# First-layer weights as three pieces of whole rows right behind the first chunk pair, one half-row pair, and a new order of all steps

## The chip, the cores and the metric

The kernel runs on one core of one Trainium2 chip. The metric is device time in microseconds. Three runs of the kernel before gave 149.23, 148.55 and 149.03 us; their median, 149.03 us, is the time before.

## The reference

Two layers are fused. The first is a linear attention with a decaying state: 4 batches, 8 heads, 768 time steps, head width 48.

```python
for t in range(S):
    cur = einsum('bhd,bhe->bhde', u * k[t], v[t])
    y[:, :, t] = einsum('bhd,bhde->bhe', r[t], state + cur)
    state = w * state + einsum('bhd,bhe->bhde', k[t], v[t])
```

Its output, laid out as x with 4 x 768 rows of 384 columns, goes through a layer norm and two dense layers with a residual:

```python
xn = (x - mean(x)) / sqrt(var(x) + 1e-06) * g_ln
out = x + maximum(xn @ w_ch1, 0) @ w_ch2      # 384 -> 1536 -> 384
```

All inputs and the output are float32; the matrix products run in bf16.

## The kernel before

The 3072 rows are cut into 24 chunks of 128 time steps, six to a batch. Two neighbouring chunks form a pair (12 pairs). The recurrence is turned into matrix products within a chunk, with a state `Z` carried from chunk to chunk.

The program is a list of steps, `PLAN`, written out by hand. Each entry is a step's name, its number and a letter for the engine (v is DVE, s is ACT, g is POOL, - stands where the step's engine is fixed). Every engine works through its own steps strictly in the order of this list, and so does the queue of SP, which issues nearly all loads and stores. Which engine waits for which data follows from the list and from the number of buffers (`SLOTS`).

The steps that matter here:

- `LK2`, `LR2`, `LV2` load a pair of k, r or v (384 KB) so that two neighbouring time steps lie in one row; `LK`, `LR`, `LV` load one chunk (192 KB). For the first `PAIRS` pairs the whole attention works on pairs laid out in such half rows (`AT2`, `Y2`, `AM2`), later pairs on single chunks (`AT`, `Y`, `AM`).
- `LN` takes the logarithm of the decay w on ACT, `WBM` spreads it over the partitions on PE, and `FR2`, `FK2`, `FR`, `FK` make tables of decay powers from it with Exp on ACT. `TL` loads an ACT table set that holds both functions: `nc.scalar.preload_act_table_set("natural_log_exp_and_others")`.
- `SK`, `SR` (and `SKH`, `SRH`, `SR2`) multiply k and r by the decay powers; `TRk`, `TRr` transpose them on PE (the pairs from number 4 on by DMA, `TDk`), `TCk`, `TCr` copy the results out of PSUM; `AT` makes the scores, `AM` masks them on DVE, `S` updates the state, `Y` gives the chunk's output, `X` completes it, `XN` normalises, `LT` and `XT` (or `LTD`, by DMA) transpose it.
- `LW1` loads the first layer's weights, `SW` scales a third of a third of them by the norm's gain into bf16 tiles `w1_sb[n][kc]`. `IW2` loads the second layer's weights on POOL's own queue. `UP` is a block of first-layer products (12 matmuls for a single chunk, 6 wide ones for a double one), `RL` the relu that takes it out of PSUM (two buffers `hp`), `DN` a third of a chunk's second-layer products, `OT` the residual, `STO` the store.
- `RS` makes the norm's factor of a chunk: on POOL with a power, or on ACT with Ln and then Exp (lines 613 and 614).
- `DU` are matmuls on zeros that feed nothing.

A tile `w1_f[n]` holds the columns of one third n of the hidden units, for all three blocks kc of the 384 input columns, so `UP,n` of a single chunk needs the one load `LW1,n`.

Of the kernel before, what the change touches and what calls it, by code (L numbers as in the profile page):

```python
# [7 lines left out]
FP32 = mybir.dt.float32  # L8
# [11 lines left out]
LN,0,s MI2,0,g MP,5,g MP,3,g WBM,0,- MP,4,g LG,0,- MM,0,g LV2,0,- DU,4096,- UWR,0,v FR2,0,s MI,0,g FR2,1,s LR2,2,- SRH,0,v  # L20
FK2,0,s SRH,1,v FK2,1,s SKH,0,v LK,5,- FK,0,s TRr,0,- SKH,1,v DU,1024,- TCr,0,s SR2,1,v TRk,0,- LR2,3,- DU,512,- SK2,1,v COL,0,-
TCk,0,s TRr,1,- LV2,1,- CV2,0,s UW,0,v Q2,0,v AT2,0,- DU,1536,- FR,0,s TCr,1,v LK,4,- WL,0,s SR2,2,g AM2,0,v S,0,- AT2,1,-
LK,6,- CC2,0,s DU,512,- ZU,0,v TRk,1,- AM2,1,v DU,512,- VB2,0,g S,1,- TCk,1,s LK,7,- DU,512,- TRr,2,- LW1,1,- SR2,3,v DU,512,-
Y2,1,- TCr,2,s LW1,2,- LV,5,- Q2,1,v Y2,0,- SK,4,g ZU,1,v UGC,0,s LV,4,- CV2,1,s X,1,v TRr,3,- SK,5,g X,0,v DU,512,-
AT2,3,- TCr,3,s DU,512,- AM2,3,v SK,7,g S,2,- XN,1,s AT2,2,- XN,0,g CC2,1,v ZU,2,v SQ,1,s DU,512,- VB2,1,g TRk,2,- AM2,2,v
S,3,- LW1,0,- TCk,2,s DU,512,- SK,6,v LT,1,- Y2,2,- SQ,0,s SW,5,g XT,1,v SW,3,s LV,6,- LT,0,- SW,4,v TRk,3,- Q2,2,g
ZU,3,v DU,1024,- SW,6,s LK,8,- XT,0,v Y2,3,- SW,7,s TCk,3,v X,2,v SW,8,s AT,5,- AT,4,- X,3,v XN,2,g DU,512,- UP,2,-
AM,5,v XN,3,s IW2,0,g LV,7,- UP,1,- RL,2,s Q2,3,g AM,4,v LT,2,- CV2,2,s DU,512,- UP,17,- RL,1,s XT,2,v S,4,- RL,17,s
LR2,4,- UP,34,- SW,0,v SW,2,s AT,6,- CC2,2,v ZU,4,v SW,1,s VB2,2,g AT,7,- AM,6,v LK,9,- Y,4,- RL,34,s UP,0,- IW2,1,g
X,4,v UP,18,- RL,0,s AM,7,v IW2,2,g Y,5,- XN,4,s LT,3,- UP,32,- RL,18,s RS,1,g LV,8,- X,5,v LT,4,- UP,33,- RL,32,s  # L30
XT,3,v XN,5,g DU,512,- CV2,3,v LV,9,- UP,16,- RL,33,s XT,4,v SK,8,v S,6,- DN,0,- SR2,4,v CC2,3,s RL,16,s UP,48,- SQ,5,s
ZU,6,v UP,64,- VB2,3,v RL,48,s TRr,4,- SQ,3,s Y,6,- SK,9,g DN,1,- RS,3,s X,6,v RL,64,s UP,66,- RS,0,g TDk,4,- SQ,2,s
DN,2,- RS,2,g LT,5,- S,7,- OT,0,v RL,66,s UP,49,- XN,6,s XT,5,v UP,50,- RL,49,v TCr,4,s LR2,6,- DN,4,- ZU,7,v UP,80,-
ZD,7,v LK,10,- CV2,4,g RL,50,v Y,7,- RL,80,s DN,5,- X,7,v LV,13,- DN,6,- Q2,4,v XN,7,s UP,65,- SQ,4,s OT,1,v LV,11,-
AT,8,- SQ,6,s SR2,6,v AT,9,- DN,8,- RS,6,s LR2,5,- AM,8,v RS,4,s DN,9,- SQ,7,s LK,11,- S,8,- DN,10,- ZU,8,v LV,10,-
UP,82,- CC2,4,s OT,2,v VB2,4,g LK,12,- LT,6,- AM,9,v Y,8,- RL,82,s DN,12,- STO,0,- RL,65,s SK,10,g DN,13,- XT,6,v LK,13,-
X,8,v DN,14,- ZD,8,g LV,12,- S,9,- UP,96,- OT,3,v SK,11,g ZU,9,v UP,98,- RL,96,s SR2,5,v Y,9,- TDk,5,- SQ,8,s DN,16,-
CV2,5,v LT,7,- TRr,5,- SK,12,v DN,17,- X,9,v TCr,5,s RL,98,v LK,15,- UP,97,- XN,9,g LK,14,- XT,7,v ZD,9,g UP,81,- RL,97,s
LR2,7,- XN,8,s SK,13,g UP,112,- RL,81,s LTD,8,- DN,18,- RS,7,s Q2,5,v TRr,6,- OT,4,v UP,114,- SK,15,g TCr,6,s RL,112,v STO,1,-
S,10,- CV2,6,g DN,20,- CC2,5,s TDk,6,- RL,114,s SK,14,v AT,10,- RS,5,s AT,11,- ZU,10,v DN,21,- SR2,7,g AM,10,v UP,113,- STO,3,-  # L40
DN,22,- AM,11,v RL,113,s TDk,7,- Y,10,- VB2,5,g UP,129,- OT,5,v TRr,7,- RL,129,s LR,19,- UP,130,- ZD,10,g X,10,v UP,133,- LV,14,-
# [29 lines left out]
def kernel(  # L71
# [31 lines left out]
    const = ctx.enter_context(tc.tile_pool(name="const", bufs=1))  # L103
# [82 lines left out]
    g_neg = const.tile([P, CK], FP32, name="g_neg")  # L186
    WLZ = const.tile([P, HP, E2], FP32, name="WLZ")
    uwI = const.tile([P, HP, 2], BF16, name="uwI")
    w1_f = [const.tile([P, CK, FW], FP32, name=f"w1_f{n}") for n in range(NW)]
    w1_sb = [[const.tile([P, FW], BF16, name=f"w1_sb{n}_{kc}") for kc in range(CK)] for n in range(NW)]  # L190
    w2_sb = [const.tile([P, FK // NW, C], BF16, name=f"w2_sb{n}") for n in range(NW)]
    w1_src = moe_w_ch1.rearrange("(kc p) (n f) -> p n kc f", p=P, n=NW)
    w2_src = moe_w_ch2.rearrange("(n p fk) c -> p n fk c", p=P, n=NW)

    psum = {}
# [135 lines left out]
                func=ACT.Exp, scale=float(L),  # L331
            )

    def LW1(n, e):
        nc.sync.dma_start(out=w1_f[n][:], in_=w1_src[:, n])

    def SW(i, e):
        n, kc = divmod(i, CK)
        o, s = w1_sb[n][kc][:], w1_f[n][:, kc]
        g = g_neg[:, kc : kc + 1]  # L340
        if e == "s":
            nc.scalar.activation(out=o, in_=s, func=ACT.Copy, scale=g)  # L342
        elif e == "v":
            nc.vector.tensor_scalar(out=o, in0=s, scalar1=g, scalar2=None, op0=ALU.mult)
        else:
            nc.gpsimd.tensor_scalar(out=o, in0=s, scalar1=g, scalar2=1.0, op0=ALU.mult, op1=ALU.mult)
# [436 lines left out]
```

## Time and profile before

| what | value |
|---|---|
| median of three runs | 149.03 us |
| span of the profiled execution | 147.5 us |
| PE busy | 141.5 us (96%) |
| DVE busy | 112.3 us (76%) |
| ACT busy | 82.4 us (56%) |
| POOL busy | 72.0 us (49%) |
| moved by DMA | 27.18 MB |
| granted TensorE clock | 1.000 |

The profile gives the span of the execution that it recorded, 147.5 us from the first to the last instruction, and no time of its own for what lies around it; the median is 1.53 us above that span. A busy PE in this profile is not PE at its peak: overlapping matmuls count as one busy stretch, and the matmuls on zeros count too.

### The profile page before, as it was taken

Reading aid. Unit: us, or ns where it says so; the run is one execution under the profiler, and the core shown is the slowest. Engines: PE = TensorE matmul, PEld = TensorE weight load, DVE = VectorE, ACT = ScalarE, POOL = GpSimd, SP = SyncE. Lnnn points to the kernel's source line nnn. Section 1 sums busy time; section 2 is a strip of 40 time slices with the busy share of each in tenths; the row PEclk is TensorE's granted clock in tenths of the full one; section 3 lists DMA queues with packets and bytes.
Section 4 is the critical chain, followed back from the end, with each engine's and each line's share of the span. In section 5 each row is a group of like instructions: output and inputs, shape, how many; then the busy total and the mean of one; then the engine's idle time right before and its main releaser. Section 6 shows DMA issues by size and latency. Waiting matters only on the chain.

```text
span 147.5 us, 4689 instructions
## 1 busy us (share of the span) xinstructions
PE 141.5 (96%) x1943; PEld 111.1 (75%) x1943; DVE 112.3 (76%) x206; ACT 82.4 (56%) x181; POOL 72.0 (49%) x96
## 2 busy tenths in 40 slices
PE   7899999799999999999999999999999999999991
PEld 3375767699987788787778787778877777878881
DVE  3499999889559887998989999499644886851642
ACT  4657783986977737736766543115795164537010
POOL 7507687984070475794854194627129330614000
PEclk9999999999999999999999999999999999999999
DMA  4999997999959899999899997998959894213023
GB/s 112 300 242 240 192 339 187 283 243 215 220 95 231 202 225 165 264 205 258 164 192 196 195 235 124 173 204 227 197 112 191 182 142 154 82 46 119 8 99 111
DMA packets 85097, 27.18 MB, mean 184 GB/s; under 512 B 80338, under 2 KB 83540, under 8 KB 85076
## 3 DMA queue, kind: packets, MB, share of 16 engines
q1 hardware_dynamic: 84642, 25.70, 78.3%
q0 software_dynamic: 432, 1.18, 4.3%
q8 instruction: 15, 0.25, 0.7%
q14 instruction: 6, 0.05, 0.1%
q10 hardware_dynamic: 2, 0.00, 0.0%
HBM read 18.88 MB, written 4.72 MB: 160 GB/s over the span
## 4 chain that ended last, share of the span: by engine, by line
PE 65%; SPq 13%; DMA 11%; DVE 6%; POOL 1%; issue 1%; DVEq 0%
PE o L674 28%; PE hp L646 25%; DMA kf<-in_k_dram 6%; DMA w_f<-in_moe_w_ch_dram 5%; SPq L374 4%; SPq L352 3%; PE at L544 3%; PE y L583 2%; SPq L358 2%; PE y L481 2%; PE y L575 2%; SPq L371 1%; SPq L377 1%; DVE hT L664 1%; PE y L460 1%
## 5 line engine op out<-in xcount | busy, mean ns | idle before, releaser
L646 PE MATMUL hp<-xT,w_sb 128*128 128x128 bf16 (+1 forms) x648 | 57.1, 237 | 0.8 <-ACT w_sb L342 0.7
L662 ACT ACTIVATE hT<-hp 128x512 bf16<-128x512 f32 x55 | 32.4, 594 | 40.5 <-PE hp L646 39.7
L646 PEld LDWEIGHTS <-w_sb 128*128 128x128 bf16 x648 | 49.3, 114 | 5.1 <-ACT w_sb L342 1.3
L674 PE MATMUL o<-w_sb,hT 128*128 128x384 bf16 x276 | 53.0, 326 | 0.0
L674 PEld LDWEIGHTS <-hT 128*128 128x128 bf16 x276 | 25.0, 97 | 12.0
L553 DVE TENSOR_TENSOR A<-at,mask 128x1024 bf16<-128x1024 f32 x20 | 24.2, 1216 | 2.1 <-PE at L544 2.1
L492 POOL TENSOR_TENSOR Vb<-vf,cc 128x768 f32<-128x768 f32 x11 | 16.5, 1498 | 14.9 <-ACT cc L200 8.5
L730 DVE SCALAR_TENSOR_TENSOR ot<-o,rs,x 128x384 f32<-128x384 f32 x23 | 14.1, 615 | 12.3 <-PE o L674 7.0
L205 POOL TENSOR_TENSOR sk<-kf,Fk 128x384 bf16<-128x384 f32 x13 | 13.6, 1053 | 8.5 <-DMA kf<-in_k_dram 7.9
L597 ACT ACTIVATE sqj<-x,sm 128x384 bf16<-128x384 f32 x24 | 14.6, 609 | 2.2 <-DVE x L590 2.2
L205 POOL TENSOR_TENSOR Z<-ZS,WLZ 128x384 bf16<-128x384 f32 x8 | 8.0, 1002 | 15.4 <-DVE ZS L565 15.4
L590 DVE SCALAR_TENSOR_TENSOR x<-y,Vb 128x384 f32<-128x384 f32 x20 | 11.0, 552 | 4.5 <-PE y L583 4.1
L664 DVE TENSOR_SCALAR hT<-hp 128x512 bf16<-128x512 f32 x17 | 11.5, 684 | 3.4 <-PE hp L646 3.3
L279 PE MATMUL o<-warm 128*128 128x512 bf16 x33 | 11.3, 427 | 1.0 <-DVE warm L228 1.0
L200 ACT COPY trr<-at 128x512 bf16<-128x512 bf16 (+1 forms) x13 | 9.1, 764 | 4.4 <-PE at L400 4.4
L205 DVE TENSOR_TENSOR sr<-rf,Fr 128x768 bf16<-128x768 f32 (+1 forms) x11 | 9.5, 870 | 1.6 <-DMA rf<-in_r_dram 1.6
L205 POOL TENSOR_TENSOR sr<-rf,Fr 128x384 bf16<-128x384 f32 (+1 forms) x5 | 6.6, 1325 | 7.0 <-DMA rf<-in_r_dram 7.0
L604 ACT ACTIVATE xn<-x,sm 128x384 bf16<-128x384 f32 x13 | 7.8, 609 | 2.3 <-DVE x L590 2.3
L606 POOL TENSOR_SCALAR xn<-x,sm 128x384 bf16<-128x384 f32 x8 | 5.3, 665 | 7.6 <-DVE x L590 7.5
L205 DVE TENSOR_TENSOR q<-trk,trr 128x1024 bf16<-128x1024 bf16 x9 | 7.5, 837 | 1.4 <-ACT xn L604 1.0
L481 PE MATMUL y<-vv,sk 128*128 128x96 bf16 (+1 forms) x96 | 7.3, 204 | 0.3 <-ACT vv L200 0.2
L205 DVE TENSOR_TENSOR sk<-kf,Fk 128x384 bf16<-128x384 f32 (+1 forms) x10 | 7.4, 747 | 0.0
(97 smaller groups left out, 179.4 us busy)
## 6 DMA issues: line engine op xcount, KB each, us to landing
out_dram<-ot SPq DMA_DIRECT2D x23, 192.0 KB, 2.6
kf<-in_k_dram SPq DMA_DIRECT2D x20, 192.0 KB, 4.2
vf<-in_v_dram SPq DMA_DIRECT2D x20, 192.0 KB, 4.3
rf<-in_r_dram SPq DMA_DIRECT2D x9, 384.0 KB, 4.7
w_f<-in_moe_w_ch_dram SPq DMA_DIRECT2D x3, 768.0 KB, 8.6
w_sb<-in_moe_w_ch_dram POOLq DMA_DIRECT2D x3, 384.0 KB, 6.0
rf<-in_r_dram SPq DMA_DIRECT2D x6, 192.0 KB, 4.3
kf<-in_k_dram SPq DMA_DIRECT2D x2, 384.0 KB, 4.5
```

What stands on the lines that cost most here:

```text
L205: engines[e].tensor_tensor(out=out, in0=in0, in1=in1, op=ALU.mult)
L279: nc.tensor.matmul(out=warm_ps[0][:].rearrange("p (a t) -> p a t", a=4), lhsT=warm[:], rhs=rhs, start=True, stop=True)
L481: nc.tensor.matmul(out=t[:, q * E2 : (q + 1) * E2].rearrange("p (e d) -> p e d", e=2), lhsT=lhs, rhs=rhs, start=first, stop=True, skip_gro ...
L492: engines[e].tensor_tensor(out=Vb2(g).rearrange("p (x h d) -> p x h d", x=2, h=H), in0=vals, in1=cc2(g)[:].unsqueeze(3).to_broadcast([P, 2 ...
L553: nc.vector.tensor_tensor(out=AA(i)[:].rearrange("p e q t -> p (e q) t"), in0=psum["at", i][:].rearrange("p e q t -> p (e q) t"), in1=mask ...
L590: nc.vector.scalar_tensor_tensor(out=xx(i)[:], in0=psum["y", i][:, :C], scalar=1.0, in1=Vb(i), op0=ALU.mult, op1=ALU.add, accum_out=sm[i][:],)
L597: nc.scalar.activation(out=sqj[:], in_=xx(i)[:], func=ACT.Square, bias=sm[i][:], scale=-float(C), accum_out=sq[g][:, j : j + 1])
L646: nc.tensor.matmul(out=t[:, a * gw : (a + 1) * gw], lhsT=w1_sb[n][kc][:, fb::FB], rhs=xT(g)[:, :size, kc, :], start=(kc == 0), stop=(kc == ...
L662: nc.scalar.activation(out=o, in_=s, func=ACT.Relu)
L664: nc.vector.tensor_relu(out=o, in_=s)
L674: nc.tensor.matmul(out=psum["o", i][:, :C], lhsT=hT(g)[:, fk, j * P : (j + 1) * P], rhs=w2_sb[d][:, a, :], start=(fk == 0), stop=(fk == FK ...
L730: nc.vector.scalar_tensor_tensor(out=ot(i)[:], in0=psum["o", i][:, :C], scalar=rs[g][:, j : j + 1], in1=xx(i)[:], op0=ALU.mult, op1=ALU.add,)
```

## The change

Three things change. The first-layer weights are cut by input block kc instead of by hidden third n: each of the three loads fetches 128 whole rows of 1536 values, 768 KB as before, and `SW` takes its third out of such a piece. Each `UP` now needs all three loads. `PAIRS` becomes 1, so pair 1 (chunks 2 and 3) uses the steps for single chunks. And the whole list of steps is replaced.

```diff
-PAIRS = 2
+PAIRS = 1
 PLAN = """
-WF,0,s MP,1,g LK2,0,- MW,0,v ML,0,v MM2,0,g DU,3072,- UF,0,- TL,0,s MO,0,v MZ,0,v LR2,0,- LR2,1,- MP,2,g MP,0,g LK2,1,-
...
+MI,0,g MW,0,v MO,0,v DU,3072,- WF,0,s MI2,0,g MP,3,g MP,1,g MP,5,g MM,0,g MZ,0,v ML,0,v LN,0,s WBM,0,- FR2,1,s FK2,1,s MP,0,g
...
-    w1_f = [const.tile([P, CK, FW], FP32, name=f"w1_f{n}") for n in range(NW)]
+    w1_f = [const.tile([P, F], FP32, name=f"w1_f{kc}") for kc in range(CK)]
...
-    w1_src = moe_w_ch1.rearrange("(kc p) (n f) -> p n kc f", p=P, n=NW)
+    w1_src = moe_w_ch1.rearrange("(kc p) f -> p kc f", p=P)
...
-    def LW1(n, e):
-        nc.sync.dma_start(out=w1_f[n][:], in_=w1_src[:, n])
+    def LW1(kc, e):
+        nc.sync.dma_start(out=w1_f[kc][:], in_=w1_src[:, kc])
...
-        o, s = w1_sb[n][kc][:], w1_f[n][:, kc]
+        o, s = w1_sb[n][kc][:], w1_f[kc][:, n * FW : (n + 1) * FW]
```

Line numbers of the changed kernel are one lower than those of the kernel before from the list of steps on (646 becomes 645).

What the new list does at the places that the prediction speaks of:

**The queue of SP around the weights.** Tiles kf, rf and vf hold k, r and v, `w_f` the first-layer weights. Before:

```order
L352 DMA kf_72<-in_k_dram 128x8x48 x2
L335 DMA w_f_224<-in_moe_w_ch_dram 128x3x512
L335 DMA w_f_225<-in_moe_w_ch_dram 128x3x512
L358 DMA vf_79<-in_v_dram 128x8x48 x2
L335 DMA w_f_223<-in_moe_w_ch_dram 128x3x512
```

Now:

```order
L351 DMA kf_70<-in_k_dram 128x8x48
L357 DMA vf_78<-in_v_dram 128x8x48 x2
L334 DMA w_f_224<-in_moe_w_ch_dram 128x1536
L334 DMA w_f_225<-in_moe_w_ch_dram 128x1536
L334 DMA w_f_223<-in_moe_w_ch_dram 128x1536
L373 DMA rf_75<-in_r_dram 128x8x96
L351 DMA kf_71<-in_k_dram 128x8x48 x2
```

The weights now follow chunks 0 to 3 (and r of pair 1) at once. Before, r of pairs 2 and 3, k of chunks 4 to 7 and, ahead of the third piece, v of chunks 4 and 5 stood in front of them.

**The start of POOL.** Two of the three loads of the second-layer weights (`w_sb`) move to POOL's first constants, the first of them eight rows ahead of this piece; the third follows after the cast of v. `sr` and `sk` are the multiplied r and k, `Vb` the bonus term, `vv` v in bf16. Before, these rows of POOL held no load. Now:

```order
L265 MEMSET sk_84 128x16x16
L265 MEMSET sk_83 128x16x16
L348 DMA w_sb_237<-in_moe_w_ch_dram 128x1536
L204 TENSOR_TENSOR sr_86<-rf_74,Fr_209 128x16x48
L204 TENSOR_TENSOR sk_83<-kf_70,Fk 128x8x48 x2
L491 TENSOR_TENSOR Vb_112<-vf_77,cc_102 128x768
L201 CAST vv_89<-vf_78 128x768
L348 DMA w_sb_235<-in_moe_w_ch_dram 128x1536
```

None of the three waits for anything but its place in POOL's row. Before, all three stood behind the first `UP`.

**ACT's table loads.** At the start `TL` no longer stands ahead of `LN`, so the built program carries one table load in front of the Ln and another in front of the first Exp (`FR2`). Further loads stand around the norm's factors of chunks 2 and 4. `hT` is the relu (`RL`), `trr` the copy of the transposed r, `rs` the factor. Before there is no table load here:

```order
L597 ACTIVATE sqj,sq_171<-x_120,sm_147 128x384
L613 ACTIVATE rs_190<-sq_171,epsc 128x1
L614 ACTIVATE rs_190<-rs_190 128x1
L613 ACTIVATE rs_188<-sq_169,epsc 128x1
L614 ACTIVATE rs_188<-rs_188 128x1
L597 ACTIVATE sqj,sq_172<-x_121,sm_148 128x384
```

Now:

```order
L199 COPY trr_95<-at 128x2x256 x2
L612 ACT_TABLE_LOAD
L612 ACTIVATE rs_188<-sq_169,epsc 128x1
L613 ACT_TABLE_LOAD
L613 ACTIVATE rs_188<-rs_188 128x1
L661 ACTIVATE hT_133<-hp 128x4x128
L230 ACT_TABLE_LOAD
L661 ACTIVATE hT_134<-hp 128x4x128
```

The same two loads stand at the factor of chunk 2. The last row but one is `TL`, which now comes here; behind it there are no more table loads. The built program has seven on ACT, where it had one.

PE's own row moves too: before, `TRr` and `TRk` of pairs 2 and 3 and the scores of chunks 4 and 5 stood ahead of the first `UP`. Now `UP` of chunks 0 and 1 starts first, with `TRr,2` behind the fourth `UP`, and the rest of these between later ones; `LT,2` moves the other way, ahead of the first `UP`. The `DU` matmuls fall from 33 to 24.

More of the change, by code (lines that the diff above doesn't have):

```diff
@@ L22 @@
[L22 to L26, printed above, removed]
@@ L32 @@
[L32 to L36, printed above, removed]
@@ L37 @@
[L37 to L41, printed above, removed]
@@ new lines @@
+CV2,0,s S,0,- CC2,0,s AM2,1,v AM2,0,v TRr,1,- DU,1024,- TRk,1,- ZU,0,v S,1,- ZU,1,v UGC,0,s TCr,1,s TCk,1,s FR,0,s Y2,1,-
+VB2,0,g Q2,1,v AT,2,- CV2,1,g AT,3,- S,2,- CC2,1,s AM,2,v IW2,0,g SW,7,g ZU,2,v Y2,0,- S,3,- SW,4,s SW,1,s VB2,1,g X,1,v X,0,v
+ZU,3,v AM,3,v DU,1536,- Y,2,- SQ,1,s XN,0,s SQ,0,s LT,0,- XN,1,s XT,0,s SW,2,g SW,5,g X,2,v SW,0,v XN,2,s DU,1024,- LT,1,- Y,3,-
+SW,3,s XT,1,s LT,2,- UP,0,- RL,0,s X,3,v XN,3,v UP,1,- LT,3,- UP,16,- RS,1,g SR2,2,g SK,5,g RL,1,s XT,2,v XT,3,v RL,16,s UP,17,-
@@ new lines @@
+TRr,2,- UP,33,- SK,4,g RL,17,v RL,33,v SW,6,v SW,8,s UP,32,- DN,0,- TRk,2,- DN,1,- RL,32,s TCr,2,s UP,2,- RL,2,s TCk,2,v Q2,2,v
+AT,4,- AT,5,- UP,34,- UP,18,- AM,4,v CV2,2,v AM,5,v SK,6,v SR2,3,g RS,0,g LK,9,- LK,7,- LV,9,- SK,9,g RL,34,s SK,7,g LV,7,-
+LK,12,- LR2,4,- LK,8,- DN,2,- S,4,- OT,0,v ZU,4,v RL,18,s SQ,3,s SQ,2,s RS,2,s CC2,2,s UP,49,- TRr,3,- UP,50,- RL,50,s RL,49,s
+LK,10,- LV,8,- STO,0,- LV,10,- LV,12,- Y,4,- TCr,3,v VB2,2,v X,4,v XN,4,v TRk,3,- DN,8,- DN,9,- DN,10,- TCk,3,v Y,5,- LT,4,-
```

70 lines of the change are left out of this document (38 added, 32 removed).

## The prediction

> **What bounds the kernel now.** I read the page's busy times first, then busy times by stretch, then the chain of work that ended last, and then the first 45 us in order of time.
>
> Busy time by stretch of the kernel before (columns: PE, PE's weight loads, DVE, ACT, POOL, then clock, DMA share, GB/s):
>
> ```profile
> 0.97:26.10 25.13, 24.09 (x418) 15.40 (x419) 20.48 (x43) 16.88 (x30) 15.18 (x30) 1.00 0.94 238
> 26.10:43.70 17.60, 16.82 (x284) 14.92 (x284) 13.30 (x27) 14.86 (x31) 11.29 (x16) 1.00 0.99 216
> 43.70:78.06 34.36, 34.36 (x481) 27.68 (x481) 30.92 (x55) 20.74 (x51) 19.51 (x18) 1.00 1.04 211
> 78.06:83.21 5.15, 5.06 (x52) 3.75 (x50) 5.15 (x10) 3.42 (x9) 1.48 (x1) 1.00 0.95 178
> 83.21:144.40 61.19, 61.19 (x712) 49.35 (x712) 41.93 (x76) 26.52 (x62) 24.13 (x29) 1.00 0.67 148
> ```
>
> From 43.7 us to 144.4 us PE never rests, apart from a detour at 78 us where DVE is busy throughout (5.15 of 5.15 us). The chain in order of time names the full-rate price of each kind of block there:
>
> ```profile
> 46.20 0.67 PE hp L646 x12
> 46.87 0.55 PE at L544 x16
> ...
> 48.83 0.18 PE y L460 x8
> 49.01 0.19 PE y L481 x4
> 49.20 0.65 PE o L674 x4
> ...
> 50.52 0.17 PE at L631 x3
> 50.69 0.17 PE y L575 x4
> 50.86 0.20 PE y L583 x8
> ...
> 55.71 0.45 PE at L400 x8
> ```
>
> So UP is 0.67 us, scores of a pair 0.55, S 0.37, DN 0.65, LT 0.17, Y 0.37 and TR 0.45. Between 26.10 and 43.70 the list of before has 14 UP (9.4), 4 DN (2.6), three S (with one more state product, about 1.1), three Y (1.1), one pair of scores (0.55), four LT (0.7) and a TR (0.45): 15.9 of 17.6 us. PE is thus the bound from the first UP on, with 1.7 us lost. Ahead of it the opposite holds: 24 us of busy time, much of it matmuls on zeros, while DMA runs at 0.94 and the chain goes through SP's queue and the weights:
>
> ```profile
> 15.90 7.37 DMA w_f<-in_moe_w_ch_dram
> 23.37 0.49 DVE w_sb L344
> ```
>
> The span is therefore the time of the first UP, plus the PE work still to do then, plus PE's stalls, plus a tail of 3.1 us (147.5 less 144.4) whose steps stay. I sum against the span of 147.5 us; the median of the runs, 149.03, is 1.53 higher, and I carry that difference over unchanged.
>
> **The change part by part. First the weights.** The first UP of before, and what fed it:
>
> ```profile
> 19.57 5.58 SPq L335 DMA_DIRECT2D w_f<-in_moe_w_ch_dram  x1
> 23.29 0.72 ACT L342 ACTIVATE w_sb<-w_f,g_neg 128x512 bf16<-128x512 f32 x1 [0.94 <-DMA w_f<-in_moe_w_ch_dram]
> 23.44 0.97 POOL L346 TENSOR_SCALAR w_sb<-w_f,g_neg 128x512 bf16<-128x512 f32 x1 [0.94 <-DMA w_f<-in_moe_w_ch_dram]
> 26.10 0.25 PE L646 MATMUL hp<-xT,w_sb 128*128 128x128 bf16 x1
> 29.41 0.87 DVE L344 TENSOR_SCALAR w_sb<-w_f,g_neg 128x512 bf16<-128x512 f32 x1
> DMA to landing us min/median/max: 7.4/8.6/9.8
> ```
>
> The last row is that of the `w_f` tiles: the third piece, issued at 19.57, took the 9.8 us and landed at 29.4. Up to and including it SP had queued eight pair loads (8 x 384 KB), six chunk loads (6 x 192 KB) and 3 x 768 KB, 6528 KB or 6.68 MB, from 0.72 us on: 233 GB/s. In the new order four pair loads, four chunk loads and the weights make 4608 KB or 4.72 MB, which at 233 GB/s lands at 21.0. But POOL's loads of the second weights now run at the same time:
>
> ```profile
> q0 software_dynamic: 432, 1.18, 4.3%
> w_sb<-in_moe_w_ch_dram POOLq DMA_DIRECT2D x3, 384.0 KB, 6.0
> 27.03 0.78 POOL L349 DMA_DIRECT2D w_sb<-in_moe_w_ch_dram  x1
> ```
>
> 4.3% of 147.5 us on all engines is 6.3 us, 2.1 us each. Two are issued among POOL's constants and certainly go ahead: 25.2. With all three ahead it is 27.3; with none felt, 21.0. I take 25.2, since the third waits on POOL for a cast of v that itself comes late. The advantage of before, that UP,2 needs one piece alone, is gone: it started 3.3 us ahead of the third landing. Now POOL must still scale its share (0.97) and PE start: 26.5, **0.4 us later** than 26.10; ends -3.8 and +2.5. Whole rows of the same bytes I cost at the same rate; a quicker transfer lies within these ends.
>
> Attention of chunks 0 to 3 must be done by then. Its start moves back, because the table load no longer hides behind the arrival of w and a second one follows:
>
> ```profile
> 1.26 1.28 ACT L231 ACT_TABLE_LOAD   x1 [1.26 <-PEq L767]
> 2.55 0.52 ACT L284 ACTIVATE ln_all<-w_row 1x384 f32<-1x384 f32 x1
> 4.81 1.05 ACT L298 ACTIVATE Fr<-hp,pow 128x384 f32<-128x384 f32 x2 [1.73 <-PE hp L288]
> ```
>
> 2 x 1.28 puts the decay powers at about 7.4 instead of 4.81. I cost this at nothing: the weights land 18 us later and cover it. If they come by 21, this chain is what is late next, and UP cannot start before about 23. Singles instead of a half-row pair for chunks 2 and 3 save PE work before the first UP, where PE idles: nothing either.
>
> **Second, work that moves behind the first UP.** TRr and TRk of pairs 2 and 3 (4 x 0.45) and the scores of chunks 4 and 5 (0.55) filled PE's wait before and now stand where PE is full; LT,2 (0.17) goes the other way: **+2.2 us**. TRr,2 needs r of pair 2, now behind all the weights: it lands near 27 and POOL multiplies it by 29.5 (1.81 us in the row below), while PE, after four UP and an LT (2.85), arrives at 29.4: just in time, so anything later shows.
>
> ```profile
> 12.15 1.81 POOL L205 TENSOR_TENSOR sr<-rf,Fr 128x768 bf16<-128x768 f32 x1 [6.44 <-DMA rf<-in_r_dram]
> ```
>
> **Third, five table loads behind the first UP**, 5 x 1.28 = 6.4 us on an ACT that is busy 14.9 of 17.6 us (stretch table). Prices around them:
>
> ```profile
> 39.27 0.29 ACT L613 ACTIVATE rs<-sq,epsc 128x1 f32<-128x1 f32 x1
> 39.59 0.20 ACT L614 ACTIVATE rs<-rs 128x1 f32<-128x1 f32 x1
> 41.33 0.60 ACT L662 ACTIVATE hT<-hp 128x512 bf16<-128x512 f32 x1 [0.46 <-PE o L674]
> 42.33 1.34 ACT L200 COPY trr<-at 128x512 bf16<-128x512 bf16 x2
> ```
>
> At chunk 2 two loads, Ln, Exp, a small copy and a relu take 3.9 us, queued ahead of the relus of UP,50 and UP,49. PE has Y, TRk, three DN, Y and LT (3.3 us) before it needs the buffer, and TRk,3 waits for a late k anyway: I cost it at nothing. At chunk 4 the relu of UP,66 waits behind the copy of trr (1.34), two loads, Ln and Exp (3.05) and takes 0.60, 5.0 us after TRr,4. PE has S (0.37), UP (0.67), two DN (1.30) and Y (0.37) until DN,18 needs that relu: 2.7. **+2.3 us** of stall. TL's 1.28 us behind it I leave to the next two blocks. Ends for all five: nothing, if ACT runs ahead of PE, and 6.4, if every load delays a relu. I take 2.3, the walk through the rows.
>
> Here the Trainium skill (ScalarE: Activation LUTs, What ACT_TABLE_LOAD costs) speaks against the change more strongly: it says a switch costs 1283 ns and another 1380 ns of drain, 2.66 us. This trace agrees on the load (1.28), but the Ln starts 0.01 us after it ends, with nothing in flight before; a load in mid-stream no run here shows. By the page two more drains would stand before that relu, and the sum would be some 2.8 us higher.
>
> **Sum:** 0.4 + 2.2 + 2.3 = 4.9 us; span 152.4, median 149.03 + 4.9 = **153.9 us**. All favourable ends give -1.6 (147.4), all unfavourable +11.1 (160.1).
>
> **The rivals.** *Early weights (faster).* If SP's loads are not delayed by POOL's and land at 21.0, the first UP starts 3.8 us earlier. Chunks 2 and 4 then come while ACT still waits for PE, of which before has plenty:
>
> ```profile
> ACT hT L662 <- PE hp L646: 39.7, 29, 6.7
> ```
>
> The loads would hide and the sum is -3.8 + 2.2 = -1.6: 147.4. It decides only from a landing before 21.9 on, where the gain exceeds the moved 2.2 us by 0.75. Against it: DMA is at 0.94 with POOL's queue empty. 0.11.
>
> *Paid back later (no change).* Before loses 3.7 us at 78 us and up to 1.7 us before 43.7; if the new order meets DVE less tightly there, PE catches up and 4.9 less 3.7 to 5.4 ends at 148.5 to 150.2, 149.5 say. For it: DVE is the busy engine there. Against: a late PE makes DVE late too. 0.10.
>
> *Every table load on the path (slower still).* 0.4 + 2.2 + 6.4 = 9.0: 158.0. For it: PE has only two buffers for UP, so a late relu stops it after two blocks. 0.12.
>
> *A cold PE (slower).* Nine matmuls on zeros fewer leave longer gaps while data is awaited. The trace shows two speeds, though it reports a granted clock of 1.00 for both:
>
> ```profile
> 0.97 2.74 PE L279 MATMUL o<-warm 128*128 128x512 bf16 x6 [0.97 <-DVE warm L228]
> 4.55 1.89 PE L279 MATMUL o<-warm 128*128 128x512 bf16 x8
> ```
>
> 0.46 against 0.24 us each. If a gap near 24 us sends PE back for as long as the slow start lasted (some 3.5 us), that costs half, 1.7 us: 155.6. 0.07. The Trainium skill (TensorE: Matmul & The Clock Gate, Part 1) names such a gate, half clock after an idle window of about 3.4 us; the trace agrees on a slow start of about that length and shows no idle window so long.
>
> **How the numbers follow.** The forecast, with 0.60, covers about 151 to 156.5. A measurement of this kernel tells 0.5% (0.75 us) from no change, so slower holds 0.60 + 0.12 + 0.07 and a little of the paid-back case, 0.81; within 0.5% 0.08, faster 0.11. The range runs from 149.0, which leaves out the early weights, to 157.8, which leaves out the worst table loads: 149.0 to 157.8. The forecast's own range is 151 to 156.5.
>
> **What would show it.** Right: seven table loads on ACT of 1.28 us; the third `w_f` landing near 25, the first L645 matmul near 26.5; an idle PE of about 2 us ahead of the third DN of chunk 4, released by the relu on ACT; PE ending near 149. Wrong: a landing by 22, table loads that begin while ACT would idle anyway, or a stretch behind 60 us with fewer stalls than the 3.7 us of before.

## The result and the profile after

| | before | after |
|---|---|---|
| median | 149.13 us (4 runs) | 161.72 us (4 runs, 161.43 to 162.90) |
| span of the profiled execution | 147.5 us | 159.6 us |
| ratio | | 1.0875, 95% interval 1.0816 to 1.0934 |

The change costs 12.6 us, where 4.9 were forecast: the direction held, and the time lies above the range. Line numbers of the changed kernel are one lower than before (645 is UP, 673 DN, 661 the relu on ACT). Fast executions of one kernel differ by up to 2.4 us (159.89 to 162.29 in experiment 13), slow ones lie higher (the kernel before reached 155.26), and the medians below are over both, the ratios over the fast ones alone. A difference below 2.4 us between two experiments is therefore told together with its place in the traces.

The engines and the clock of the page after (busy us and share; then the clock in 40 slices of 4 us):

```profile
PE 144.0 (90%) x1854; PEld 112.9 (71%) x1854; DVE 116.4 (73%) x201; ACT 87.5 (55%) x188; POOL 83.7 (52%) x102
PEclk9999999999999969999999999999999999999999
```

PE has about as much to do as before (144.0 against 141.5), but its share falls from 96% to 90%, and one slice near 56 us shows a low clock. Busy time by stretch of the kernel after, in the columns of the prediction's table (PE's is the first after the length of the stretch):

```profile
0.97:25.19 24.22, 22.04 (x286) 13.18 (x286) 16.02 (x31) 16.24 (x32) 16.36 (x34) 1.00 0.98 251
25.19:47.10 21.91, 18.35 (x289) 15.66 (x290) 17.04 (x27) 13.80 (x27) 11.59 (x10) 1.00 0.94 202
47.10:63.80 16.70, 13.85 (x176) 11.15 (x175) 11.47 (x21) 12.10 (x23) 8.01 (x7) 0.90 0.95 186
63.80:84.30 20.50, 18.72 (x274) 15.68 (x272) 16.67 (x27) 13.14 (x31) 13.14 (x13) 1.00 0.54 124
84.30:156.35 72.05, 71.08 (x838) 57.20 (x835) 54.57 (x97) 32.23 (x78) 34.29 (x34) 1.00 0.77 149
```

Length less PE's busy time gives PE's idle time behind the first UP: 3.56 + 2.85 + 1.78 + 0.97 = 9.16 us. The prediction's table gives for before 17.60 - 16.82 = 0.78 us up to 43.70, and next to nothing behind it, 0.09 us in all of the rest up to 144.40:

```profile
43.70:144.40 100.70, 100.61 (x1242) 80.78 (x1241) 77.99 (x138) 50.69 (x121) 45.11 (x48) 1.00 0.81 171
```

Before thus idles 0.87 us in all. In the kernel after, the clock of 0.90 over 16.70 us takes another 1.7. The 12.1 us of span therefore divide into: first UP 0.9 earlier (25.19 for 26.10), 8.3 more idle, 1.7 at half clock, 0.15 more tail, and by difference 2.9 of PE work that now stands behind the first UP. The waits of PE after (total us, times, longest):

```profile
PE o L673 <- ACT hT L661: 2.8, 1, 2.8
PE y L574 <- ACT cc L199: 1.9, 1, 1.9
PE y L574 <- DVE x L589: 1.7, 2, 1.3
PE at L399 <- POOL sr L204: 1.0, 1, 1.0
```

**The two costly stops are both table loads.** In order of time, chunk 2 and then chunk 4 (start, length, engine, instruction, and in brackets the idle time before it and what ended it; rows between these are left out):

```profile
37.66 1.28 ACT L612 ACT_TABLE_LOAD   x1
39.27 1.28 ACT L613 ACT_TABLE_LOAD   x1
40.67 0.15 ACT L199 COPY cc<-y 128x16 f32<-128x16 f32 x1
40.88 0.33 PE L574 MATMUL y<-Z,trr 128*128 128x96 bf16 x4 [1.95 <-ACT cc L199]
```

```profile
51.77 0.76 ACT L199 COPY trr<-at 128x512 bf16<-128x512 bf16 x1
52.55 1.28 ACT L612 ACT_TABLE_LOAD   x1
53.84 0.29 ACT L612 ACTIVATE rs<-sq,epsc 128x1 f32<-128x1 f32 x1
54.15 1.28 ACT L613 ACT_TABLE_LOAD   x1
55.55 0.58 ACT L661 ACTIVATE hT<-hp 128x512 bf16<-128x512 f32 x1
56.19 0.82 PE L673 MATMUL o<-w_sb,hT 128*128 128x384 bf16 x4 [2.83 <-ACT hT L661]
```

At chunk 2 the last thing behind the loads that PE needs is not a relu but the copy `cc`, 0.15 us long: it empties the one buffer `y`, into which the first products of `Y` (r times the state, L574) go next. At chunk 4 it is the relu, as forecast.

**Later, DVE is late where POOL multiplies**, with a stop of PE that before did not have. The scaling of the state (Z, step `ZD`) takes 2.31 us beside POOL's product q; behind it stand Vb and x in DVE's row, and PE waits for x:

```profile
74.43 2.13 POOL L204 TENSOR_TENSOR q<-trk,trr 128x1024 bf16<-128x1024 bf16 x1 [3.89 <-ACT trr L199]
74.66 2.31 DVE L204 TENSOR_TENSOR Z<-ZS,WLZ 128x384 bf16<-128x384 f32 x1
78.57 0.33 PE L574 MATMUL y<-Z,trr 128*128 128x96 bf16 x4 [1.28 <-DVE x L589]
```

### The profile page after: what moved, and what is told of

Read it like the earlier page. It is cut to its first block, busy times and chain, and to the rows that moved or that the text cites. A ratio compares the mean times of both kernels' runs of the same rounds, so it can differ in the third digit from the quotient of the medians.

```text
span 159.6 us, 4521 instructions
## 1 busy us (share of the span) xinstructions
PE 144.0 (90%) x1854; PEld 112.9 (71%) x1854; DVE 116.4 (73%) x201; ACT 87.5 (55%) x188; POOL 83.7 (52%) x102
## 4 chain that ended last, share of the span: by engine, by line
PE 53%; DVE 13%; SPq 10%; DMA 9%; ACT 7%; issue 4%; POOL 2%; DVEq 0%; ACTq 0%
PE hp L645 22%; PE o L673 21%; DMA rf<-in_r_dram 7%; DVE A L552 3%; DMA xT<-xn 3%; PE at L543 2%; SPq L357 2%; SPq L217 2%; DVE Z L204 2%; DVE Vb L491 2%; POOL sr L204 2%; SPq L351 2%; ACT L613 2%; ACT L612 2%; PE y L582 2%
## 5 line engine op out<-in xcount | busy, mean ns | idle before, releaser
L661 ACT ACTIVATE hT<-hp 128x512 bf16<-128x512 f32 x54 | 31.5, 594 | 37.4 <-PE hp L645 37.1
L552 DVE TENSOR_TENSOR A<-at,mask 128x1024 bf16<-128x1024 f32 x22 | 26.7, 1216 | 0.0
L204 POOL TENSOR_TENSOR sr<-rf,Fr 128x768 bf16<-128x768 f32 (+1 forms) x11 | 18.8, 1705 | 9.8 <-DMA rf<-in_r_dram 7.3
L491 POOL TENSOR_TENSOR Vb<-vf,cc 128x768 f32<-128x768 f32 x9 | 13.4, 1488 | 17.6 <-ACT cc L199 14.9
L204 POOL TENSOR_TENSOR sk<-kf,Fk 128x384 bf16<-128x384 f32 x17 | 17.4, 1031 | 3.8 <-DMA kf<-in_k_dram 1.9
L615 POOL TENSOR_SCALAR rs<-sq 128x1 f32<-128x1 f32 (+1 forms) x9 | 2.4, 270 | 17.8 <-ACT sqj L596 17.2
L204 POOL TENSOR_TENSOR q<-trk,trr 128x1024 bf16<-128x1024 bf16 x3 | 6.6, 2189 | 7.8 <-ACT trr L199 3.9
L574 PE MATMUL y<-Z,trr 128*128 128x96 bf16 x76 | 6.3, 205 | 4.0 <-ACT cc L199 1.9
L574 PEld LDWEIGHTS <-trr 128*128 128x128 bf16 x76 | 5.1, 97 | 5.9 <-issue 5.0
L582 PE MATMUL y<-vv,A 128*128 128x48 bf16 x176 | 8.1, 185 | 0.0
L199 ACT COPY trr<-at 128x512 bf16<-128x512 bf16 x10 | 6.7, 753 | 1.8 <-PE at L399 1.8
```

The lines of the kernel that those rows point to most:

```text
L204: engines[e].tensor_tensor(out=out, in0=in0, in1=in1, op=ALU.mult)
L491: engines[e].tensor_tensor(out=Vb2(g).rearrange("p (x h d) -> p x h d", x=2, h=H), in0=vals, in1=cc2(g)[:].unsqueeze(3).to_broadcast([P, 2 ...
L552: nc.vector.tensor_tensor(out=AA(i)[:].rearrange("p e q t -> p (e q) t"), in0=psum["at", i][:].rearrange("p e q t -> p (e q) t"), in1=mask ...
L574: nc.tensor.matmul(out=t[:, q * E2 : (q + 1) * E2], lhsT=trr(i // 2)[:, i % 2, q, :], rhs=ZZ(i - 1)[:, q, :], start=first, stop=True, skip ...
L582: nc.tensor.matmul(out=t[:, h * D : (h + 1) * D], lhsT=AA(i)[:, par, q, :], rhs=vv(i)[:, h, :], start=first, stop=True, skip_group_check=True,
L661: nc.scalar.activation(out=o, in_=s, func=ACT.Relu)
```

## Experiments

Each kernel was timed against the kernel before on the same chip, whose medians were 148.83 to 150.77. The first four are two pairs: two parts of the change undone in the new order, two parts done alone in the old one.

**1. One table load, in the new order.**

```diff
-... MZ,0,v ML,0,v LN,0,s ... UP,81,- TL,0,s RL,81,s ...
+... MZ,0,v ML,0,v TL,0,s LN,0,s ... UP,81,- RL,81,s ...
```

> The changed kernel with the step TL put back in front of LN, so that ACT has one table load instead of seven; nothing else moves. Theory A (the loads are the main cause: they stall PE by about 2.1 us at 41 us and 3 us at 56 us, delay what hangs on them, and make PE cold for 3.4 us): 7 to 9 us come back, 153 to 155 us. Theory B (the loads cost what the prediction gave them, 2.3 us, and the rest of the 12.6 us is the new order itself): 159 us.

Measured: 159.09 us (156.63 to 159.73), ratio 1.0605 (1.0455 to 1.0755), 2.6 us less than after. The six loads are gone, and a new stop stands in the head, the part ahead of the first `UP` (PE in order of time, then the clock of the page):

```profile
15.35 0.80 PE L480 MATMUL y<-vv,sk 64*128 64x96 bf16 x8 [4.74 <-ACT vv L199]
PEclk9998555999999999999999999999999999999999
```

Without the loads in the head PE is ready for the products of k and v in the first state update (`S`, L480) at 10.6 us, but v of that pair, issued at 4.89 us, lands at 14.5 beside POOL's two early loads of 384 KB (in experiment 5, without them, at 9.1), and PE runs at half clock behind the wait. The first `UP` starts at 29.07 instead of 25.19. Three of the four executions have this clock (0.957); the one at 1.000 took 156.63 us. So part of the gain was turned into a wait for data.

**2. The seven table loads alone, in the old order.**

```diff
-... UF,0,- TL,0,s MO,0,v ... RS,6,s LR2,5,- ...
+... UF,0,- MO,0,v ... RS,6,s TL,0,s LR2,5,- ...
```

> The kernel before with the step TL moved from the start to behind the norm's factor of chunk 6, so that ACT gets seven table loads, two of them ahead of the decay powers and four around the factors of chunks 3 and 6. Theory A: 5 to 8 us slower, 154 to 157 us. Theory B: 2 to 3 us slower, 151 to 152 us.

Measured: 153.69 us (152.60 to 158.26), ratio 1.0307 (1.0227 to 1.0387). The loads alone cost 4.9 us between the medians (4.6 by the ratio). Behind the second pair of loads PE is stopped by the same 0.15 us copy as after at chunk 2:

```profile
57.84 0.33 PE L575 MATMUL y<-Z,trr 128*128 128x96 bf16 x4 [2.47 <-ACT cc L200]
```

The granted clock is 0.967 in this trace and 0.997 to 1.000 in the other three executions (152.60 to 154.05 us), so the 4.9 us hold next to no half clock.

**3. The second-layer weights late, in the new order.**

```diff
-... AT2,1,- IW2,1,g MM2,0,g ... IW2,2,g SR2,1,g ... AM,2,v IW2,0,g ... RS,1,g ...
+... AT2,1,- MM2,0,g ... SR2,1,g ... AM,2,v ... IW2,0,g IW2,1,g IW2,2,g RS,1,g ...
```

> The changed kernel with the three loads of the second-layer weights put behind the scaling of the first-layer weights on POOL. Theory C (the early second weights hold up k, r, v and the first weights): the third piece of the first weights lands near 21 instead of 24.6 us and 2 to 3 us come back, 159 us. Theory D (they only trade places with data that is needed later, and the first second-layer products then wait for them): no gain, 161 to 163 us.

Measured: 161.63 us (160.96 to 162.27), ratio 1.0865 (1.0798 to 1.0931): no gain. The third piece of `w_f` lands at 21.4 us instead of 24.6, so POOL's loads do delay it as the prediction took it, but the first UP comes at 24.53 instead of 25.19, since the attention chain ahead of it, late by the head's table loads, is now the later one (without them, in experiment 5, it is done at 22.99); and the 2.84 us stop at chunk 4 stays.

**4. Whole rows alone, in the old order.** The change's own diff of `w1_f`, `w1_src`, `LW1` and `SW`, and in the list the third load joins the other two:

```diff
-... LW1,2,- LV,5,- ... S,3,- LW1,0,- TCk,2,s ...
+... LW1,2,- LW1,0,- LV,5,- ... S,3,- TCk,2,s ...
```

> The kernel before with nothing changed but the first-layer weights: three pieces of whole rows, issued one after the other where the first two pieces stood. By the prediction's transfer rate the third piece lands near 27.5 us and the first UP starts near 28.5 instead of 26.1: 1 to 2.5 us slower, 150.5 to 151.5 us. If whole rows move faster than rows of 512 values, no change.

Measured: 152.34 us (151.84 to 153.48), ratio 1.0245 (1.0151 to 1.0338). Each `UP` now needs the third piece, which lands at 25.9; PE waits, and the clock falls to half for 6.8 us:

```profile
27.34 0.29 PE L646 MATMUL hp<-xT,w_sb 128*128 128x128 bf16 x1 [1.55 <-ACT w_sb L342]
PEclk9999999659999999999999999999999999999998
```

**5. Experiments 1 and 3 together.** The diffs of 1 and 3 on the same list.

```diff
-... ML,0,v LN,0,s ... IW2,1,g MM2,0,g ... RS,1,g ...
+... ML,0,v TL,0,s LN,0,s ... MM2,0,g ... IW2,0,g IW2,1,g IW2,2,g RS,1,g ...
```

> The changed kernel with TL in front of LN and, besides, the three loads of the second-layer weights put behind the scaling of the first-layer weights. With TL alone in front, PE waited 4.7 us for v of the first pair, which the second weights had delayed to 14.5 us, and then ran cold for 13.7 us. Theory E (that cold stretch is the price of the early second weights once the loads are out of the way): PE stays warm, 154.5 to 156.5 us. Theory D (the second weights only trade places with other data): 157 to 160 us.

Measured: 157.75 us (157.22 to 158.13), ratio 1.0540 (1.0482 to 1.0599). The weights land at 19.5 us and the first UP starts at 22.99, 3.1 us ahead of before. The lead is gone before 40 us, since the chunks behind the weights come late:

```profile
35.48 0.33 PE L480 MATMUL y<-vv,sk 128*128 128x96 bf16 x4 [1.99 <-DVE vv L201]
```

v of chunks 4 and 5 lands at 33.8 and 34.5, and a stretch of 3.41 us at half clock follows, which costs another 1.7 us. With the loads and the early transfers gone, 8 us remain.

**6. Three table loads, all in the head.**

```diff
-... TCk,1,s FR,0,s Y2,1,- ... UP,81,- TL,0,s RL,81,s ...
+... TCk,1,s FR,0,s TL,0,s Y2,1,- ... UP,81,- RL,81,s ...
```

> The changed kernel with TL put behind FR (the last Exp of the start), so that the two table loads of the start stay and the four around the factors of chunks 2 and 4 go. Theory A (those four cost the 2.8 us lost near 41 us and the 4.6 us lost near 56 us, the cold PE behind the second included): 153.5 to 155.5 us. Theory B (2.3 us): 159 us.

Measured: 158.96 us (157.67 to 159.41), ratio 1.0610 (1.0538 to 1.0681). Four loads fewer in mid-stream give back 2.8 us of the 6.5 that the trace of after shows around them (1.95 + 2.83 + 1.7); 1.6 us are taken back at the first UP, which waits 1.37 us for the weights and starts at 26.78 instead of 25.19, and 1.7 by the half clock that follows it from 27.15 to 30.56. That leaves 3.2.

**7. As 6, with q of pair 6 on DVE and the state update of chunk 10 on POOL.**

```diff
-... ZD,10,v ... Q2,6,g ...
+... ZD,10,g ... Q2,6,v ...
```

> As the kernel with TL behind FR, and besides the product q of pair 6 on DVE instead of POOL and the scaling of the state of chunk 10 on POOL instead of DVE. In the changed kernel that scaling took 2.31 us on DVE, instead of 0.55, while POOL worked on this q. Theory F (DVE and POOL slow each other there and PE waits for it): 1 to 2 us faster than without the swap. Theory G (DVE catches up before PE needs it): no difference.

Measured: 157.30 us (156.88 to 158.57), ratio 1.0526 (1.0441 to 1.0611). The stop of 1.28 us (at 76.35 in experiment 6) is gone from the trace, and 1.7 us from the median. The clock behind the first UP is full in this trace and was not in that of 6, but that is not the gain: both reach the same product of q at 69 us (68.88 and 69.01), and a wide `UP` farther on at 104.80 instead of 106.43.

**8. One pair only, in the old order.** The steps of pair 1 as singles:

```diff
-PAIRS = 2
+PAIRS = 1
-... LK2,1,- ... SK2,1,v ... AT2,2,- ... Y2,2,- ...
+... LK,2,- LK,3,- ... SK,2,v SK,3,v ... AT,2,- ... Y,2,- ...
```

> The kernel before with PAIRS = 1: chunks 2 and 3 loaded and worked on as single chunks, each step in the place of the paired one. All of it lies ahead of the first UP, where PE has time: 148.5 to 150 us by the prediction. If rows of half the length slow the loads ahead of the weights: up to 151 us.

Measured: 151.15 us (150.76 to 152.96), ratio 1.0126 (1.0045 to 1.0206), 1.6 us: PE waits 2.52 us for Z of DVE at 24.9 us and the first `UP` starts at 28.57 instead of 26.10, so the prediction's "nothing" for this part does not hold.

**9. As 5, with v of chunks 4 and 5 earlier in SP's queue.**

```diff
-... LK,5,- LV,6,- LK,6,- LR2,3,- LV,4,- LV,5,- UWR,0,v ...
+... LK,5,- LV,4,- LV,5,- LV,6,- LK,6,- LR2,3,- UWR,0,v ...
```

> The changed kernel with one table load (TL at the front) and its second-layer weights late, as in the kernel of 157.75 us, and besides LV,4 and LV,5 (v of chunks 4 and 5) right behind LK,5 in SP's queue, ahead of v and k of chunk 6 and r of pair 3. Theory (the earlier weights starve the chunks behind them): v of chunks 4 and 5 lands near 28 instead of 34 us, PE's wait of 2 us at 35.5 us and the 3.4 us at half clock behind it (1.7 us lost) go, 154 to 155.5 us. Rival (POOL and DVE are what is late there, v only the last of several): the wait moves to the cast of v or to the next pair, 157 to 158 us.

Measured: 156.87 us (156.12 to 158.98), ratio 1.0492 (1.0375 to 1.0609). Mostly the rival: the wait moves to the next pair, whose r now comes last (PE in order of time):

```profile
37.77 0.87 PE L399 MATMUL at<-ident,sr 128*128 128x128 bf16 x8 [3.68 <-POOL sr L204]
```

**10. As 9, with the swap of experiment 7.**

```diff
-... ZD,10,v ... Q2,6,g ...
+... ZD,10,g ... Q2,6,v ...
```

> The kernel with v of pair 2 early, and besides Q2,6 on DVE and ZD,10 on POOL (where the changed kernel has POOL and DVE). Theory (what is left beside starvation is DVE operations stretched while POOL works on q at 65 to 75 us): 1.5 us below the same kernel without the swap, 152.5 to 154 us. Rival (the order of the list is late in many small places, and this one is only the first to show): within 0.7 us of it. In no theory does it reach the 148.8 us of the kernel before, since some 2 us of the moved PE work and one pair fewer (+1.6) stay.

Measured: 156.15 us (155.16 to 157.23), ratio 1.0462 (1.0354 to 1.0571). 0.7 us less: at the edge of the rival, and inside the scatter of either kernel. The traces are clearer: the stop of 1.28 us is gone here too, and from the product of q near 68 us to the same wide `UP` near 105 us PE takes 35.9 us instead of 37.4, as the theory has it.

**11. The weights early, nothing else, in the old order.** Thirds as before, the three loads right behind `LV2,0`.

```diff
-... LV2,0,- DU,4096,- ... TRr,2,- LW1,1,- ... LW1,2,- ... S,3,- LW1,0,- ...
+... LV2,0,- LW1,1,- LW1,2,- LW1,0,- DU,4096,- ... TRr,2,- ... S,3,- ...
```

> The kernel before, pieces and all other steps as they were, with the three loads of the first-layer weights moved right behind LV2,0 in SP's queue (the place they have in the changed kernel). Theory (early weights push r and k of pairs 2 and 3 behind them, and PE of this list needs those ahead of the first UP): all three pieces land by 21 us, but TRr,2 and TRk,2 come 4 to 7 us later than before, 151 to 154 us. Rival (the place is harmless, only the whole rows cost): within 0.7 us of before, or faster.

Measured: 158.13 us (156.77 to 159.71); even its fastest run is 1.7 us above the slowest of before (155.11), and the median 8.1 above its median. This list needs r of pair 2 ahead of the first UP (PE in order of time, and the clock):

```profile
22.18 1.03 PE L400 MATMUL at<-ident,sr 128*128 128x128 bf16 x8 [7.35 <-POOL sr L205]
PEclk9999755999999999999999999999999999999999
```

The second piece of `w_f` lands at 17.1 us, and none is read before 31.1. The early place of the weights, more than their shape, is the dearest part of the change unless the list is rewritten around it.

**12. As 9, with all data of chunks 4 and 5 ahead of the weights.** The list of 9, and:

```diff
-... LV,2,- LW1,1,- LW1,2,- LW1,0,- LR2,2,- LK,4,- LK,5,- LV,4,- LV,5,- ...
+... LV,2,- LR2,2,- LK,4,- LK,5,- LV,4,- LV,5,- LW1,1,- LW1,2,- LW1,0,- ...
```

> The kernel with v of pair 2 early, with LR2,2 LK,4 LK,5 LV,4 LV,5 (all data of chunks 4 and 5, 1152 KB, some 5 us at the rate seen) moved ahead of the three loads of weights. Theory (what counts is the sum of bytes ahead of each need; moving them ahead of the weights only moves the wait): first UP 4 to 5 us later, near 26.5, no wait for r, k or v of pair 2 behind it, 154 to 157 us, within 1.5 us of the kernel with v early. Rival (starvation of pair 2 is the whole of what is left): 150 to 152 us.

Measured: 159.09 us (158.20 to 160.65), ratio 1.0638 (1.0520 to 1.0755). The first UP moves to 26.3 us and the waits for pair 2 go: the wait is moved, not removed, and it ends 2.2 us worse than experiment 9, 2.1 above the range expected. Ahead of the first UP PE now waits 2.19 us for a normalised chunk, and 6.8 us at half clock follow, from 23.9 to 30.7, over the first `UP` blocks.

**13. Matmuls on zeros in the wait of chunk 4.** Twelve of 384 columns, which add zeros to the open output, ahead of `DN,18` of the changed kernel.

```diff
+    def DK(i, e):
+        for _ in range(i):
+            nc.tensor.matmul(out=psum["o", 4][:, :C], lhsT=warm[:], rhs=w2_sb[0][:, 0, :], start=False, stop=False)
-... Q2,4,v DN,18,- ...
+... Q2,4,v DK,12,- DN,18,- ...
```

> The changed kernel with 12 matmuls that add zeros to the open output of chunk 4 (384 columns, about 0.17 us each, 2.0 us) just ahead of the third DN of that chunk, where PE waits 2.83 us for the relu. Theory (the wait of 2.8 us is what brings the half clock of 3.41 us behind it): the wait falls to 0.8 us at the same end, the half clock goes, half of 3.41 is won: 159.5 to 160.3 us. Rival (the half clock has another cause, or the time is lost again at the DVE stalls behind it): within 0.7 us of 161.7.

Measured: 161.00 us (159.89 to 162.29), ratio 1.0753 (1.0644 to 1.0861), 0.7 us less than after. PE in order of time, and the clock (line numbers are four higher here):

```profile
53.16 2.11 PE L284 MATMUL o<-w_sb,warm 128*128 128x384 bf16 x12
56.16 0.82 PE L677 MATMUL o<-w_sb,hT 128*128 128x384 bf16 x4 [0.89 <-ACT hT L665]
62.81 0.33 PE L578 MATMUL y<-Z,trr 128*128 128x96 bf16 x4
70.59 0.35 PE L463 MATMUL y<-uwI,q 128*128 128x2 bf16 x8 [1.39 <-DVE q L204]
PEclk9986999999999999999999999999999999999999
```

The same places in the kernel after:

```profile
64.33 0.33 PE L574 MATMUL y<-Z,trr 128*128 128x96 bf16 x4
71.22 0.35 PE L459 MATMUL y<-uwI,q 128*128 128x2 bf16 x8 [0.50 <-DVE q L204]
```

The third DN starts at the same time (56.16 for 56.19), but the low clock behind it is gone, and at the first products of `Y` (62.81 for 64.33) PE is 1.5 us ahead. Two of the four executions have a granted clock of 1.000, none of the four of the kernel after. So the wait does cause the half clock, and it costs about 1.5 us there. (The low clock near 12 us stands ahead of the first `UP` and is not what was changed.) At 70.6 DVE makes PE wait 0.9 us longer, which leaves 0.6: gain given back at the next late engine. Theory and rival each explain one half.

**14. As 10, with the cast of v of pair 5 on ACT.** The list of 10, and:

```diff
-... CV2,5,v ...
+... CV2,5,s ...
```

> The kernel with v of pair 2 early and q on DVE (156.15 us), and besides CV2,5 (the cast of v of pair 5) on ACT instead of DVE, where it took 2.17 us beside a POOL multiplication of 2.15 us and PE then waited 1.43 us for q on DVE. Theory (the DVE operations stretched beside POOL are what stalls PE there): that wait goes, 1.0 to 1.5 us less, 154.6 to 155.2 us. Rival (POOL or ACT is late there as well): within 0.5 us.

Measured: 154.76 us (154.02 to 156.35), ratio 1.0287 (1.0169 to 1.0406). The wait for q falls from 1.27 to 0.46 us, not to nothing, since a state update on DVE is now the one stretched (2.04 us). The medians of 10 and 14 differ by 1.4 us, their profiled executions by 0.1: supported by the wait, not settled by the times.

**15. As 14, with r of pair 3 ahead of v and k of chunk 6.** The list of 14, and:

```diff
-... LV,5,- LV,6,- LK,6,- LR2,3,- ...
+... LV,5,- LR2,3,- LV,6,- LK,6,- ...
```

> The kernel with the cast on ACT, and besides LR2,3 (r of pair 3) ahead of LV,6 and LK,6 in SP's queue. Theory (the rest of the starvation is r of pair 3, for which PE waits 3.4 us at 36.8 us and then runs 6.8 us at half clock): r lands some 2 us earlier, the wait falls by about 2 us and the cold stretch by half: 2 to 4 us below the kernel with the cast on ACT, 151 to 153 us. Rival (the wait moves to v or k of chunk 6): within 0.7 us of it.

Measured: 153.49 us (151.56 to 155.19), ratio 1.0157 (1.0024 to 1.0291). The wait for that r falls from 3.83 to 0.66 us, and the half clock behind it is gone:

```profile
35.85 0.62 PE L399 MATMUL at<-ident,sr 128*128 128x128 bf16 x8 [0.66 <-POOL sr L204]
38.27 0.33 PE L574 MATMUL y<-Z,trr 128*128 128x96 bf16 x4 [1.13 <-ACT cc L199]
```

The median falls by 1.3 us, less than the 2 to 4 expected; that other stops take the rest is argued from this trace, whose execution took 155.19 us. With one table load, late second-layer weights, three loads reordered and three operations moved, the new order stands 2.7 us above the kernel before (150.77 in that comparison; 0.4 to 4.4 us by the interval of the ratio). No version tried beats it.

## Why the prediction was right or wrong

**Right: the first term, in mechanism.** The third `w_f` landed at 24.6 (25.2 in the sum), delayed by POOL's loads: without them 21.4 (experiment 3; the prediction had 21.0 for that case). The first UP came at 25.19, 1.3 us earlier than the 26.5 forecast, so the term was -0.9 and not +0.4: the landing gives 0.6 of it, and the last scaling stood on DVE (0.49 us, from 24.65) and not on POOL (0.97). The rows of `w_f` after (duration ns, first and last start; then issue to landing):

```profile
L334 SPq DMA_DIRECT2D w_f<-in_moe_w_ch_dram x3: 433/811/1195, 14.2 to 16.2; - x3
DMA to landing us min/median/max: 5.6/6.8/8.4
```

The early-weights rival fell at its condition (a landing before 21.9), and experiments 3 and 5 show that its gain would not have stood either: with the landing at 21.4 the attention chain was late, as the prediction said, though it held UP until 24.53 and not "about 23"; with 19.5 the chunks behind the weights were. The rival's -3.8, a first UP at 22.3, also broke that bound of the prediction's own.

**Right within 0.7: the moved PE work**, +2.2 forecast against 2.9, which is found by difference and not block by block. "Just in time" for TRr,2 was 1.0 us late, as the waits show.

**Wrong: the third term, +2.3 for table loads; about 6.5.** The walk through chunk 4 was good: 2.83 us of wait for the relu of the third DN. Two steps failed. "At chunk 2 ... I cost it at nothing" looked at the relus and not at the small copy in the same queue: 1.95 us. And the rival of the cold PE was tied to a gap near 24 us and given 0.07, while the forecast's own wait of 2.3 us could bring it; it cost 1.5 to 1.7. The rival with every load on the path had 6.4 us for this term, near in size but not in mechanism: two pairs of loads stopped PE, one through `cc` and one through a relu, the load of `TL` stopped nothing, and 1.7 of the 6.5 are the clock. The rule of the Trainium skill (ScalarE: Activation LUTs, What ACT_TABLE_LOAD costs) by which a switch costs a further 1380 ns of drain is not seen here either: the copy of trr ends at 52.53, the load starts at 52.55, and the Ln 0.01 us after it ends.

**Wrong: the later stretches, taken as unchanged.** No term of the sum has the other 3.5 us of idle time (8.3 - 1.95 - 2.83), in stops of up to 1.3 us, of which 1.04 is the wait for r of pair 2 above and 1.28 the one for x. The reading behind the rival "paid back later" was false too: the 3.7 us of DVE on the chain at 78 us were not lost by PE, which was busy for 5.06 of 5.15 us there. A chain that runs through another engine is no proof of an idle PE; the busy time is. Nor did before lose 1.7 us ahead of 43.70: PE idled there for 0.78, and the sum of blocks missed the rest. Before had no slack to pay anything back with. With these terms the forecast of 4.9 becomes 4.9 - 1.3 + 0.7 + 4.2 + 3.5 + 0.15 (tail) = 12.15 us of span.

**Wrong: costs of nothing.** One pair was costed at nothing and costs 1.6 us alone (experiment 8). What follows the weights in SP's queue was not priced at all beyond TRr,2, and experiments 5, 9 and 14 show waits of 2.0 to 3.8 us there as soon as PE is not already late. The table loads of the head were costed at nothing too, since the weights land 18 us later; experiment 3, where the chain releases the first UP at 24.53, shows that at most 0.7 us of that cover was left (25.19).

**The sum does not come apart into parts.** Undoing all the table loads in the new order gives 2.6 us (4.0 by the ratio), or 3.9 with the second-layer weights late (experiments 3 and 5; 4.8 by the ratio), although 6.5 of the trace stand at them; done alone in the old order, loads cost 4.9, whole rows 3.5, early weights 8.1 and one pair 1.6, 18.1 together where the change costs 12.6. PE waits for the latest of several, and each removed wait uncovers the next. What stays open is the last 2.7 us of experiment 15: its trace has waits of 0.6 to 1.1 us on seven different releasers, of which none was tried alone.

## What to carry to other kernels

Where a change adds a stall to one engine's row, ask of every instruction queued behind the stall who waits for it, the shortest ones first: a copy of 0.15 us stopped PE for 1.95. In a list without slack (PE busy 96%) a reordering is priced by the waits it may open on every engine, not by the one it names, and a PE wait of some 2 us can carry a second price at the clock, as the end of the next section works out. Bytes moved ahead in a full queue move everything behind them back; the gain at the first use is paid at the second.

## What the runs showed of the hardware

- A PE wait of 2.83 us was followed by 3.41 us at half clock in the records of the trace, and with 2.11 us of it filled by matmuls on zeros it was not (experiment 13). The Trainium skill (TensorE: Matmul & The Clock Gate, Part 1) puts the fall behind an idle window of about 3.4 us; here a shorter wait was enough, and in experiment 5 one of 1.99 us.
- A DVE state update with both operands in SBUF took 2.31 us beside a POOL multiplication of 2.13, where the median of the same shape is 0.56; in the kernel before, x, which reads one operand from PSUM, kept its 0.55 us beside the same multiplication on POOL. This agrees with the Trainium skill (SBUF — State Buffer, Who interferes with whom), which says that a DVE instruction with two SBUF inputs contends with a GpSimd instruction that reads SBUF.
- The piece of whole rows landed 5.6 to 8.4 us after its issue, the thirds of the same 768 KB before took 7.4 to 9.8; other loads ran beside both, so the runs do not show whether the rows are the cause.

The length of a wait alone does not decide about the clock: one of 1.37 us stood ahead of the half clock in experiment 6 (with shorter ones, 1.85 us idle in its step), while 1.95 us at chunk 2 and 2.52 us in experiment 8 had none behind them. In the clock records of all the traces a stretch at half clock inside the span lasts 3.41 us or two, three or four times that. Cut into such steps, the kernel after around chunk 4 and experiment 8 around its wait read (stretch, its length, PE's busy time; the clock is the third number from the end):

```profile
53.70:57.11 3.41, 0.92 (x9) 0.68 (x10) 0.93 (x3) 3.35 (x6) 3.12 (x3) 1.00 1.16 264
57.11:60.53 3.42, 3.42 (x47) 3.16 (x45) 2.71 (x5) 2.53 (x6) 0.15 (x1) 0.50 1.07 232
```

```profile
20.27:23.69 3.42, 1.71 (x21) 1.07 (x18) 3.42 (x6) 3.01 (x7) 3.32 (x4) 1.00 1.05 370
23.69:27.10 3.41, 1.59 (x25) 1.10 (x25) 2.51 (x6) 1.95 (x3) 2.67 (x2) 1.00 0.96 191
27.10:30.51 3.41, 3.20 (x61) 2.85 (x62) 2.77 (x6) 1.70 (x3) 3.13 (x3) 1.00 1.12 275
```

PE idles 2.49 us of one step in the first case, and the next step has half clock; in the second the wait is split over two steps with 1.71 and 1.82 us idle, and the clock stays. Over all the traces, each of the 14 full-clock steps with more than 1.84 us of idle PE was followed by half clock, and of those with less only two were (1.47 us in experiment 4, 0.94 in the head of experiment 2; why these two is open).
